# Grouping a head's softmax transpositions by key block instead of by query tile

## The chip, the cores and the metric

The kernel runs on one core of one Trainium2 chip. The metric is the device time of one execution in microseconds (us), lower is better; the times shown are a median of three runs. Engines: PE is TensorE's matmul side and PEld its weight loads, DVE is VectorE, ACT is ScalarE, POOL is GpSimd, SP is SyncE, which issues the DMAs.

## What is computed

A fused layer in three parts: a causal attention with a position bias (4 batches of 8 heads, 576 tokens, head width 64), a token mix with a two-layer ReLU network over it, and a second attention with 4 experts as heads (per batch), whose rows are gated by the two best experts. The change touches only what both attentions share, the way from the softmax matrix to its product with the values:

```
scores = where(causal, -1e9, scale * q @ k.T + min(bias, 0))
attn   = exp(scores - max);  attn = attn / (sum(attn) + 1e-9)
out    = attn @ v
```

## The kernel before

A head's 576 queries are cut into five **query tiles** t = 0 to 4 of 64, 128, 128, 128, 128 rows; because of the causal mask, tile t needs 64 + 128t keys (widths 64, 192, 320, 448, 576). In units of 128 keys, tile t has t full **key blocks** and one **diagonal half** of 64 keys. The softmax matrix of a head lies in a buffer P (two, used in turn by even and odd heads), its transposed form in a buffer pt (three, in turn).

The class `Attn` does both attentions. Its `run` (line 438) is a pipeline of **slots**, one per head and tile: slot i does, in this order, `qk` (PE: scores of tile i%5 of head i//5), `tr` (PE: transpositions of the head two before), `peak` (DVE: mask, negate, row extreme, PSUM to P; line 373), `exp` of the slot before (ACT; line 380), `evac` (ACT or DVE: the transposed pieces from PSUM to pt; lines 76 and 78, inside the helper `cp`), in every second slot of a head `norm` of the head before (DVE sums and reciprocals, lines 385 and 386, then POOL scales the five tiles of P in place, one instruction a tile, line 391), then a step of the product with the values (`pv`, line 432, once for each pair of heads, in the second slot after a pair's last `tr`, that is in slot 1 of an even head), and fillers: loads, conversions of weights, matmuls of the next stage.

So the transpositions of head n stand in the slots of head n+2, which overwrites the same buffer P. A group of transpositions r = 0 to 4 fills one PSUM bank (tag `t`, two banks), and the copy out of it must be done before the bank's next use, two groups later. `TRP` (line 67) says what group r holds: r = 0 is tile 1's key block and the diagonal halves of tiles 0 and 1; r = 1 is tile 2 with its half; r = 2 tile 3 with its half; r = 3 the four full blocks of tile 4; r = 4 its half. `evac` copies a group's full blocks by one instruction (scattered over t places of pt) and its halves by another: eight copies a head. `ENGA` and `ENGG` name the engine of each group, a for ACT and v for DVE: in the first attention r = 0 of even heads and r = 2 of odd heads go to DVE, in the second r = 4 of all heads, the others to ACT.

In the first attention (32 heads) the order on every engine is the program's; in the second (16 heads, counted from 0 again in names, 32 to 47 in the text) the framework's scheduler orders the instructions by its own estimates.

The first attention's operands L and R are loaded and split for each pair of heads while the pair before runs: `prep_steps` (line 580) splits the raw q and k into high and low parts on ACT and DVE (lines 489 and 492), and SP then issues DMAs that place the parts (line 462); the second low part is made in slot 2 of an even head, behind `peak` on DVE.

```
for i in slots:
    qk(i); tr(i - 10); peak(i); exp(i - 1); evac(i - 10)
    if i % 5 == 1: norm(i // 5 - 1)
    one step of pv; fillers(i)
```

Of the kernel before, what the change touches and what calls it, by code (L numbers as in the profile page):

```python
# [20 lines left out]
P = 128  # L21
NP = H // 2
NT = 5
# [6 lines left out]
I0 = [0, 64, 192, 320, 448]  # L30
WID = [64, 192, 320, 448, 576]
OFF = [0, 64, 256, 576, 1024]
# [4 lines left out]
PST = 448  # L37
# [12 lines left out]
STREAM = (((0, 0),), ((-1, 5),), ((0, 1),), ((0, 2), (1, -2)), ((-1, 6),), ((0, 3),), ((0, 4), (2, -3)), ((1, -1),))  # L50
FAST = (40, 70)

ENGA = ('vaaaaa', 'aavaav')
ULA = "gvgg"
WLE = "g"

HALVES = 152
UFIRST = 161
WIDE = (7,)
ENGG = ('aaaava', 'aaaava')  # L60

GTAB = "kkkkvvvvvqqqq......."
GATE = (9, 5, 2)
OB = "avava"
XG = 0

TRP = ((1, 0, 2), (2, 2, 3), (3, 3, 4), (4, 0, 0), (0, 4, 5))
HIENG = "av"
BG = (1, 1, 0, 2, 1)
ULF = "vggg"  # L70
# [3 lines left out]
def cp(nc, eng, out, in_):  # L74
    if eng == "a":
        nc.scalar.activation(out=out, in_=in_, func=AF.Copy)  # L76
    else:
        nc.vector.tensor_copy(out=out, in_=in_)


def free_ap(ap, off, dims):

    return bass.AP(tensor=ap.tensor, offset=ap.offset + off, ap=[list(ap.ap[0])] + [list(d) for d in dims])
# [76 lines left out]
def fused_kernel(ctx, tc, qk, v, s, u, vv, w12, wp, out):  # L160
    nc = tc.nc
    cst = ctx.enter_context(tc.tile_pool(name="cst", bufs=1))

    ident = cst.tile([P, P], F32, name="ident")
# [162 lines left out]
    class Attn:  # L327
# [65 lines left out]

        def tr(self, n, r):

            ps = self.pst.tile([P, 512], F32, tag="t", name=f"t_{n}_{r}")
            Pn = self.P[n % 2]
            t, a, e = TRP[r]  # L400
            for kb in range(t):
                c0 = OFF[t] + P * kb
                nc.tensor.transpose(ps[:, P * kb:P * kb + P], Pn[:, c0:c0 + P], ident)  # L403
            for k in range(a, e):
                c0, x = OFF[k] + WID[k] - 64, P * (t + k - a)
                nc.tensor.transpose(ps[0:64, x:x + P], Pn[:, c0:c0 + 64], ident)  # L406
            return ps

        def evac(self, n, r, ps):
            pt = self.pt[n % 3]  # L410
            t, a, e = TRP[r]
            if t:
                cp(nc, self.engines[n % 2][r], free_ap(pt[:, :], I0[t], [[PST, t], [1, P]]), ps[:, :P * t])
            if e > a:
                cp(nc, self.engines[n % 2][r], free_ap(pt[0:64], (PST + P) * a, [[PST + P, e - a], [1, 64]]),
                   free_ap(ps[0:64], P * t + 64, [[P, e - a], [1, 64]]))

        def push_pv(self, n):

# [90 lines left out]
    with ExitStack() as cx:  # L510
# [19 lines left out]

        attn = Attn((st, psq, pst), 4, ENGA)
        NH = B * H
# [387 lines left out]
    with ExitStack() as cx:  # L920
# [17 lines left out]

        attn = Attn((st, psq, pst), 4, ENGG)

# [162 lines left out]
        for n in range(B * E):  # L1103
            b, e = divmod(n, E)
# [105 lines left out]
```

## Time and profile before

| what | value |
|---|---|
| times of three runs | 869.67, 871.74, 872.11 us |
| median | 871.74 us |
| span of the profiled execution (first to last instruction) | 870.1 us |
| PE busy | 814.2 us, 94% of the span |
| DVE busy | 603.4 us, 69% |
| ACT busy | 466.9 us, 54% |
| POOL busy | 310.6 us, 36% |
| copies of transposed pieces | 304 on ACT, 80 on DVE |

The profile gives the span of the profiled execution and no other time of it; the median lies 1.6 us above that span. The first attention runs from about 10 to 307 us, the ReLU network from then to about 690 us, the second attention from there to the end. A duration in the profile is that of one instruction from start to end; two instructions of one engine can overlap at their ends. `x2` in a timeline row means that two instructions in a row were merged into one row.

### The profile page before, as it was taken

To read this page: it belongs to the slowest core of one execution; us is meant where nothing else is said; L and a number is where in the kernel's file an instruction comes from. 1 tells how busy PE (TensorE), PEld (TensorE's weight loads), DVE (VectorE), ACT (ScalarE), POOL (GpSimd) and SP (SyncE) were. 2 spreads that over 40 slices of the span, in tenths; PEclk is the share of its full clock that TensorE was granted. 3 is DMA by queue.
4 is the path that set the end of the run, shared out by engine and by line. 5 is a ranking of instruction groups with operands and counts; after the bars stand their busy time and mean duration, and the time that the engine had idled before them with its cause. 6 is when DMAs were issued, how large, how long until landed. Compare 5 with 4: busy or idle time off the path is not lost.

```text
span 870.1 us, 17626 instructions
## 1 busy us (share of the span) xinstructions
PE 814.2 (94%) x6068; PEld 747.8 (86%) x6068; DVE 603.4 (69%) x1759; ACT 466.9 (54%) x1384; POOL 310.6 (36%) x468
## 2 busy tenths in 40 slices
PE   3887898999999999999999999999999999999997
PEld 2665676898987889999999999999999988999875
DVE  8687788877687349985885887577446785656541
ACT  6587668866677344323442443333323567666672
POOL 5444255444334324323432342233233123232241
PEclk9898899999999999999999999999999999999999
DMA  7888479687570151111111121112000122112221
GB/s 206 224 212 213 127 187 241 165 210 194 157 195 16 56 188 37 49 50 25 53 48 48 49 61 50 49 43 57 1 1 1 30 42 43 37 55 50 67 64 61
DMA packets 36945, 79.66 MB, mean 92 GB/s; under 512 B 4792, under 2 KB 7992, under 8 KB 36856
## 3 DMA queue, kind: packets, MB, share of 16 engines
q1 hardware_dynamic: 36856, 78.53, 33.7%
q8 instruction: 48, 0.79, 0.4%
q14 instruction: 41, 0.34, 0.1%
HBM read 38.80 MB, written 8.40 MB: 54 GB/s over the span
## 4 chain that ended last, share of the span: by engine, by line
PE 72%; DVE 13%; ACT 5%; DMA 4%; issue 3%; POOL 1%; SPq 1%; DVEq 0%; POOLq 0%; ACTq 0%
PE hps L826 18%; PE facc L844 17%; PE pv L432 9%; PE qkp L1054 5%; PE t L403 4%; PE ops L1077 3%; PE facc L308 3%; PE vps L987 3%; PE qk L362 3%; PE qk L363 2%; PE hps L294 2%; DVE P L373 2%; PE t L406 2%; DMA c_raw_w<-in_w_dram 2%; DMA L<-Cd 2%
## 5 line engine op out<-in xcount | busy, mean ns | idle before, releaser
L278 POOL TENSOR_TENSOR ul<-uT,uh 128x288 fp32r<-128x288 f32 x126 | 103.8, 843 | 175.5 <-ACT uh L277 158.9
L380 ACT ACTIVATE P<-P,stat 64x64 f32<-64x64 f32 (+4 forms) x240 | 133.8, 558 | 43.4 <-DVE stat L373 39.8
L391 POOL TENSOR_SCALAR P<-P,stat 64x64 f32<-64x64 f32 (+4 forms) x160 | 100.9, 646 | 132.0 <-DVE stat L386 88.0
L373 DVE CUSTOM_DVE_ANT_0 P<-qk,mask 64x64 f32<-64x64 f32 (+4 forms) x240 | 116.4, 486 | 45.6 <-PE qk L363 28.8
L362 PE MATMUL qk<-R,L 128*128 128x288 f32 (+4 forms) x288 | 96.7, 340 | 23.1 <-DVE L L573 9.8
L830 ACT ACTIVATE hh<-hps 128x288 fp32r<-128x288 f32 x110 | 44.9, 408 | 135.2 <-PE hps L826 135.0
L76 ACT ACTIVATE pt<-t 64x64 f32<-64x64 f32 (+5 forms) x304 | 89.9, 336 | 42.0 <-PE t L406 36.6
L844 PE MATMUL facc<-hh,wh 128*128 128x288 f32 x376 | 111.2, 296 | 0.6 <-DVE aT L851 0.6
L826 PE MATMUL hps<-uh,wl 128*128 128x288 f32 x376 | 111.2, 296 | 0.0
L826 PE MATMUL hps<-ul,wh 128*128 128x288 f32 x376 | 111.1, 296 | 0.0
L826 PE MATMUL hps<-uh,wh 128*128 128x288 f32 x376 | 111.0, 295 | 0.0
L831 DVE SCALAR_TENSOR_TENSOR hl<-hps,hh 128x288 fp32r<-128x288 f32 x110 | 50.1, 455 | 87.7 <-ACT hh L830 87.4
L844 PE MATMUL facc<-hh,wl 128*128 128x288 f32 x376 | 110.9, 295 | 0.0
L844 PE MATMUL facc<-hl,wh 128*128 128x288 f32 x376 | 110.8, 295 | 0.0
L403 PE MATMUL t<-ident,P 128*128 128x128 f32 x480 | 89.6, 286 | 15.6 <-ACT pt L76 5.6
L363 PE MATMUL qk<-R,L 68*128 68x288 f32 (+9 forms) x288 | 89.1, 315 | 1.2 <-DMA L<-Cd 1.2
L391 POOL TENSOR_SCALAR P<-P,stat,pt 64x64 f32<-64x64 f32 (+4 forms) x80 | 48.5, 620 | 113.3 <-DVE stat L386 57.6
L362 PEld LDWEIGHTS qk<-R,L 128*128 128x128 f32 x288 | 57.3, 199 | 31.3 <-issue 14.9
L403 PEld LDWEIGHTS t<-ident,P 128*128 128x128 f32 x480 | 58.7, 143 | 28.9 <-issue 15.6
L432 PE MATMUL pv<-pt,V 128*64 128x288 f32 (+4 forms) x752 | 80.6, 364 | 0.0
L201 POOL TENSOR_TENSOR wl<-c_a_w,wh 128x256 fp32r<-128x256 f32 x56 | 43.6, 778 | 93.4 <-ACT wh L198 90.9
L432 PEld LDWEIGHTS pv<-pt,V 128*64 128x64 f32 x752 | 52.2, 147 | 27.8 <-issue 7.7
(194 smaller groups left out, 2196.7 us busy)
## 6 DMA issues: line engine op xcount, KB each, us to landing
c_raw_w<-in_w_dram SPq DMA_DIRECT2D x64, 256.0 KB
uT<-in_qk_dram SPq DMA_DIRECT2D x15, 576.0 KB
L<-HI SPq DMA_DIRECT2D x28, 288.0 KB
R<-HI SPq DMA_DIRECT2D x28, 288.0 KB
V<-in_v_dram SPq DMA_DIRECT2D x16, 320.0 KB
R<-uT SPq DMA_DIRECT2D x14, 288.0 KB
L<-uT SPq DMA_DIRECT2D x14, 288.0 KB
aD<-stage SPq DMA_DIRECT2D x6, 576.0 KB
```

Source lines behind the costliest of these rows:

```text
L76: nc.scalar.activation(out=out, in_=in_, func=AF.Copy)
L278: eng.tensor_tensor(out=l_, in0=src, in1=h_.bitcast(F32), op=OP.subtract)
L362: nc.tensor.matmul(ps[:, bk, :w], lhsT=q1[:, rows], rhs=k1[:, c0:c0 + w], start=True, stop=False)
L363: nc.tensor.matmul(ps[:, bk, :w], lhsT=q2[:, rows], rhs=k2[:, c0:c0 + w], start=False, stop=True)
L373: nc.vector.tensor_tensor_reduce(out=po, in0=view, in1=mk, scale=-1.0, scalar=3.0e38, op0=OP.add, op1=OP.min, accum_out=stat[P - M:, 0, t: ...
L380: nc.scalar.activation(out=po, in_=po, func=AF.Exp, scale=-1.0, bias=stat[P - M:, 0, t:t + 1], accum_out=stat[P - M:, 1, t:t + 1])
L391: nc.gpsimd.tensor_scalar(out=pv, in0=pv, scalar1=stat[r0:, 2, t:t + 1], scalar2=1.0 if gate is None else gate(t)[r0:], op0=OP.mult, op1=O ...
L403: nc.tensor.transpose(ps[:, P * kb:P * kb + P], Pn[:, c0:c0 + P], ident)
L432: nc.tensor.matmul(ps[64 * hh:64 * hh + 64, half, lo - a:e - a], lhsT=V(hh, kb), rhs=pt[:, PST * kb + lo:PST * kb + e], start=kb == 0, sto ...
L826: nc.tensor.matmul(ps, lhsT=w[:, 0, cs], rhs=x, start=i == 0, stop=i == 11)
L831: nc.vector.scalar_tensor_tensor(out=hl, in0=ps, scalar=0.0, in1=hh.bitcast(F32), op0=OP.max, op1=OP.subtract)
L844: nc.tensor.matmul(accs[c][d], lhsT=w[:, 1, cs], rhs=x, start=f == fs[0] and i == 0, stop=f == fs[-1] and i == 2)
```

## The change

The groups are cut the other way. Group 0 is now the five diagonal halves, group r = 1 to 4 is key block r-1 of the tiles r to 4: 4, 3, 2 and 1 transpositions. In pt a key block's columns of the tiles behind the diagonal lie side by side, so each group leaves PSUM by one copy with one unbroken run (512, 384, 256 and 128 columns), and group 0 by one copy of 5 times 64 columns on 64 partitions. The engine of group r is the same as before. The number of transpositions of a head is the same, 15; a group has 5, 4, 3, 2, 1 of them where it had 3, 3, 4, 4, 1.

```diff
-ENGA = ('vaaaaa', 'aavaav')
+ENGA = ('vaaaa', 'aavaa')
-ENGG = ('aaaava', 'aaaava')
+ENGG = ('aaaav', 'aaaav')
-TRP = ((1, 0, 2), (2, 2, 3), (3, 3, 4), (4, 0, 0), (0, 4, 5))
...
         def tr(self, n, r):
             ps = self.pst.tile([P, 512], F32, tag="t", name=f"t_{n}_{r}")
             Pn = self.P[n % 2]
-            t, a, e = TRP[r]
-            for kb in range(t):
-                c0 = OFF[t] + P * kb
-                nc.tensor.transpose(ps[:, P * kb:P * kb + P], Pn[:, c0:c0 + P], ident)
-            for k in range(a, e):
-                c0, x = OFF[k] + WID[k] - 64, P * (t + k - a)
-                nc.tensor.transpose(ps[0:64, x:x + P], Pn[:, c0:c0 + 64], ident)
+            if r == 0:
+                for k in reversed(range(NT)):
+                    c0 = OFF[k] + WID[k] - 64
+                    nc.tensor.transpose(ps[0:64, 64 * k:64 * k + P], Pn[:, c0:c0 + 64], ident)
+            else:
+                for t in range(r, NT):
+                    c0, x = OFF[t] + P * (r - 1), P * (t - r)
+                    nc.tensor.transpose(ps[:, x:x + P], Pn[:, c0:c0 + P], ident)
             return ps
 
         def evac(self, n, r, ps):
             pt = self.pt[n % 3]
-            t, a, e = TRP[r]
-            if t:
-                cp(nc, self.engines[n % 2][r], free_ap(pt[:, :], I0[t], [[PST, t], [1, P]]), ps[:, :P * t])
-            if e > a:
-                cp(nc, self.engines[n % 2][r], free_ap(pt[0:64], (PST + P) * a, [[PST + P, e - a], [1, 64]]),
-                   free_ap(ps[0:64], P * t + 64, [[P, e - a], [1, 64]]))
+            eng = self.engines[n % 2][r]
+            if r == 0:
+                cp(nc, eng, free_ap(pt[0:64], 0, [[PST + P, NT], [1, 64]]),
+                   free_ap(ps[0:64], 64, [[64, NT], [1, 64]]))
+            else:
+                w, c0 = P * (NT - r), (PST + P) * (r - 1) + 64
+                cp(nc, eng, pt[:, c0:c0 + w], ps[:, :w])
```

How this moves the instructions, at three places. In the names, `t_14_0` is group 0 of head 14, `qk_16_1` the scores of tile 1 of head 16, `pv_13` the product of heads 12 and 13; a row without a count is one instruction. In the changed kernel a line behind the table at line 67 has a number lower by one.

PE in the first attention, slots 0 and 1 of head 16, up to the first matmul of the pair's product; before:

```order
L362 MATMUL qk_16_0_1678<-R1_0_121,L1_0_119 128x64
L363 MATMUL qk_16_0_1678<-R2_0_124,L2_0_122 128x64
L403 MATMUL t_14_0_1681<-ident_58,P0_114 128x128
L406 MATMUL t_14_0_1681<-ident_58,P0_114 64x128 x2
L362 MATMUL qk_16_1_1695<-R1_0_121,L1_0_119 128x192
L363 MATMUL qk_16_1_1695<-R2_0_124,L2_0_122 128x192
L403 MATMUL t_14_1_1698<-ident_58,P0_114 128x128 x2
L406 MATMUL t_14_1_1698<-ident_58,P0_114 64x128
L432 MATMUL pv_13_1713<-pt0_105,V_6_1388 64x288
```

and with the change:

```order
L361 MATMUL qk_16_0_1636<-R1_0_121,L1_0_119 128x64
L362 MATMUL qk_16_0_1636<-R2_0_124,L2_0_122 128x64
L400 MATMUL t_14_0_1639<-ident_58,P0_114 64x128 x5
L361 MATMUL qk_16_1_1654<-R1_0_121,L1_0_119 128x192
L362 MATMUL qk_16_1_1654<-R2_0_124,L2_0_122 128x192
L404 MATMUL t_14_1_1657<-ident_58,P0_114 128x128 x4
L431 MATMUL pv_13_1672<-pt0_105,V_6_1356 64x288
```

Nine transpositions stand ahead of the product where six stood; group 0 reads all five tiles of P where it read tiles 0 and 1.

PE behind the product, slots 2 and 3 of the same head; before:

```order
L362 MATMUL qk_16_2_1732<-R1_0_121,L1_0_119 128x320
L363 MATMUL qk_16_2_1732<-R2_0_124,L2_0_122 128x320
L403 MATMUL t_14_2_1735<-ident_58,P0_114 128x128 x3
L406 MATMUL t_14_2_1735<-ident_58,P0_114 64x128
L362 MATMUL qk_16_3_1748<-R1_0_121,L1_0_119 128x448
L363 MATMUL qk_16_3_1748<-R2_0_124,L2_0_122 128x448
L403 MATMUL t_14_3_1751<-ident_58,P0_114 128x128 x4
```

and with the change:

```order
L361 MATMUL qk_16_2_1691<-R1_0_121,L1_0_119 128x320
L362 MATMUL qk_16_2_1691<-R2_0_124,L2_0_122 128x320
L404 MATMUL t_14_2_1694<-ident_58,P0_114 128x128 x3
L361 MATMUL qk_16_3_1705<-R1_0_121,L1_0_119 128x448
L362 MATMUL qk_16_3_1705<-R2_0_124,L2_0_122 128x448
L404 MATMUL t_14_3_1708<-ident_58,P0_114 128x128 x2
```

One transposition fewer in slot 2, two fewer in slot 3. Tile 2 of P, which `peak` of `qk_16_2` overwrites, is last read by group 2 now, in the same slot; before it was last read by group 1.

DVE in the second attention, slots 0 to 3 of head 45 (`qk_13`), with the sum and the reciprocal for head 44's `norm` (`stat0`); before:

```order
L373 ISA P1_8993,stat1_8987<-qk_13_0_10898,mask_63 64x64
L373 ISA stat1_8987 64x1
L373 ISA P1_8993,stat1_8987<-qk_13_1_10909,mask_63 128x192
L373 ISA stat1_8987 128x1
L373 ISA P1_8993,stat1_8987<-qk_13_2_10927,mask_63 128x320
L373 ISA stat1_8987 128x1
L385 TENSOR_SCALAR stat0_8985<-stat0_8985 128x5
L373 ISA P1_8993,stat1_8987<-qk_13_3_10939,mask_63 128x448
L373 ISA stat1_8987 128x1
L386 RECIPROCAL stat0_8985<-stat0_8985 128x5
```

and with the change:

```order
L372 ISA P1_8897,stat1_8891<-qk_13_0_10769,mask_63 64x64
L372 ISA stat1_8891 64x1
L384 TENSOR_SCALAR stat0_8889<-stat0_8889 128x5
L372 ISA P1_8897,stat1_8891<-qk_13_1_10781,mask_63 128x192
L372 ISA stat1_8891 128x1
L385 RECIPROCAL stat0_8889<-stat0_8889 128x5
L372 ISA P1_8897,stat1_8891<-qk_13_2_10799,mask_63 128x320
L372 ISA stat1_8891 128x1
L372 ISA P1_8897,stat1_8891<-qk_13_3_10809,mask_63 128x448
L372 ISA stat1_8891 128x1
```

The scheduler now puts the reciprocal ahead of the scores of tiles 2 and 3; at the same place of head 35, for head 34, its order is the same as before.

## Rows read from the trace of the kernel before

**Rows 1.** Engines by stage: stretch, length, busy us (instructions) by engine, PEclk, DMA share, GB/s.

```profile
10.00:160.00 150.00, 124.07 (x838) 97.04 (x839) 122.00 (x408) 112.16 (x358) 69.70 (x105) 0.92 0.78 201
160.00:295.00 135.00, 131.34 (x1047) 117.37 (x1047) 100.13 (x325) 90.17 (x283) 55.55 (x86) 1.00 0.54 145
...
690.00:725.00 35.00, 32.27 (x244) 29.56 (x244) 26.96 (x104) 24.20 (x76) 11.71 (x20) 1.00 0.17 35
725.00:820.00 95.00, 94.83 (x742) 86.62 (x739) 56.43 (x199) 61.58 (x184) 26.49 (x48) 1.00 0.20 51
820.00:870.00 50.00, 43.07 (x291) 33.48 (x289) 18.09 (x60) 26.59 (x82) 12.48 (x22) 1.00 0.20 60
```

**Rows 2.** Chain of waits, first attention, three places: start us, length us, what.

```profile
58.35 5.94 DMA L<-uT
...
133.14 4.19 DMA L<-Cd
...
138.59 2.92 PE pv L432 x32
...
142.86 0.45 PE t L403 x4
...
146.31 4.34 DMA L<-Cd
...
150.74 0.27 PE qk L363
```

**Rows 3.** Timeline of DVE, slot 2 of head 16; in brackets idle time before, releaser.

```profile
142.15 0.49 DVE L373 CUSTOM_DVE_ANT_0 P<-qk,mask 128x320 f32<-128x320 f32 x1 [0.65 <-POOL P L391]
...
142.56 0.83 DVE L492 SCALAR_TENSOR_TENSOR uT<-uT,half,HI 128x576 fp32r<-128x576 f32 x1
```

**Rows 4.** Copies out of PSUM, by form (busy us, mean ns) and from timelines.

```profile
L76 ACT ACTIVATE pt<-t 128x512 f32<-128x512 f32 x48 | 28.1, 586 | 4.2 <-PE t L403 4.1
...
L76 ACT ACTIVATE pt<-t 128x384 f32<-128x384 f32 x32 | 15.6, 487 | 31.6 <-PE t L406 31.5
...
155.81 0.59 ACT L76 ACTIVATE pt<-t 128x384 f32<-128x384 f32 x2 [0.52 <-PE t L406]
...
L78 DVE COPY pt<-t 128x384 f32<-128x384 f32 x16 | 8.8, 551 | 3.4 <-PE t L406 3.4
...
77.93 0.68 DVE L78 COPY pt<-t 128x384 f32<-128x384 f32 x2
```

**Rows 5.** Timelines: POOL's five scalings and PE's group 0, of heads 4, 14, 34, 44.

```profile
48.81 2.90 POOL L391 TENSOR_SCALAR P<-P,stat 64x64 f32<-64x64 f32 x5 [6.36 <-ACT pt L76]
...
50.46 0.30 PE L403 MATMUL t<-ident,P 128*128 128x128 f32 x1
...
134.81 3.12 POOL L391 TENSOR_SCALAR P<-P,stat 64x64 f32<-64x64 f32 x5 [2.85 <-DVE stat L386]
...
137.51 0.33 PE L403 MATMUL t<-ident,P 128*128 128x128 f32 x1
...
717.98 3.10 POOL L391 TENSOR_SCALAR P<-P,stat,pt 64x64 f32<-64x64 f32 x5 [8.20 <-ACT pt L76]
...
720.30 0.30 PE L403 MATMUL t<-ident,P 128*128 128x128 f32 x1 [0.82 <-POOL P L391]
...
828.12 3.10 POOL L391 TENSOR_SCALAR P<-P,stat,pt 64x64 f32<-64x64 f32 x5 [9.55 <-DVE stat L386]
...
829.76 0.30 PE L403 MATMUL t<-ident,P 128*128 128x128 f32 x1 [0.82 <-POOL P L391]
```

**Rows 6.** Timeline of DVE: scores of tile 3 of head 45, ahead of head 44's reciprocal.

```profile
827.13 0.63 DVE L373 CUSTOM_DVE_ANT_0 P<-qk,mask 128x448 f32<-128x448 f32 x1 [0.18 <-PE qk L363]
```

**Rows 7.** Two stretches of Rows 1's view, and the product that the chain has there.

```profile
70.00:80.00 10.00, 7.42 (x56) 6.07 (x53) 8.61 (x30) 7.64 (x25) 5.54 (x10) 1.00 0.98 260
80.00:90.00 10.00, 7.95 (x48) 5.17 (x47) 5.54 (x20) 4.44 (x15) 4.81 (x8) 0.66 0.68 170
...
83.45 5.53 PE pv L432 x32
```

## The prediction

> **What bounds the kernel now.** First the stretches [rows 1], to see which engine is full in which stage. In the second attention between 725 and 820 us PE works 94.83 of 95 us, in the first attention between 160 and 295 us 131.34 of 135: there PE sets the time, and copies on ACT (61.58 and 90.17 us) lie beside it. From 10 to 160 us nobody is full: PE 124 of 150, DVE 122, ACT 112. So there I read the chain of waits. Three times it goes the same way [rows 2]: the pair's product (138.59 us, 2.92 us long), the scores and transpositions behind it, then a DMA that brings the operands of the next pair (146.31, 4.34 us), then the first scores of that pair (150.74), which waited for it; the other two such DMAs are those at 58.35 and 133.14. What joins product and DMA is on DVE [rows 3]: the scores of tile 2 come at 142.15 after 0.65 us of idling, and the split whose result the DMA carries stands right behind them, at 142.56. The row puts the idling down to POOL, but POOL's scaling of that buffer had ended at 134.81 + 3.12 = 137.93 [rows 5]; the chain has PE there. So in this stretch a pair of heads pays for whatever stands on PE ahead of the scores of slot 2.
>
> The sum is made against the profiled execution, whose span is 870.1 us; the median of the three runs is 871.74, and a difference is carried over to it. A measurement here tells 0.3%, 2.6 us, from no change.
>
> **The copies that go.** 48 heads lose three copies each; 16 even and 16 odd heads of the first attention lose two on ACT and one on DVE, 16 of the second three on ACT: 112 on ACT, 32 on DVE. What one is worth is less than its length, since it starts before the one ahead of it ends. On ACT the pair of 384 and 64 columns takes 0.59 us; one copy of 448 columns would lie between 487 and 586 ns, about 537 [rows 4]: 0.05 us saved, 112 x 0.05 = 5.6 us of ACT. On DVE the pair takes 0.68, the 384 columns left of it 0.551: 0.13 us in each odd head; in even heads a copy of 128 and one of 2 x 64 columns become one of 5 x 64, which I take for even. That is 2 x 2 x 0.05 + 0.13 = 0.33 us for a pair of heads. From 160 to 295 us and from 725 to 820 us PE covers it: nothing. From 10 to 160 us there are about 8.5 pairs: 2.8 us if all of it were on the path, 0 if none; since chain pieces of PE and DMA hold most of that path I take 1.0. In the last two heads, which PE no longer covers (43.07 of 50 us) [rows 1], 6 x 0.05 = 0.3. **Together -1.3 us, bounds -3.1 and 0.**
>
> The Trainium skill (Perfetto Trace Analysis, Optimizing Scalar/DVE Operations) says that an instruction of these engines carries some 51 ns (ScalarE) or 125 ns (VectorE) of access to PSUM, and that grouping pays where the engine is saturated. The ACT figure agrees with the 0.05 us above; by the page's figures an estimate of what is freed is 112 x 0.051 + 32 x 0.125 = 9.7 us of engine time. Whether it pays is the second half of the rule, and by rows 1 no ACT or DVE is full; were they the bound, the third rival below would be the forecast.
>
> **The transpositions that come earlier.** Their number stays, so PE's work stays. But nine instead of six stand ahead of the product and of the scores of slot 2. Four take 0.45 us [rows 2], 0.11 each, so product and scores come 0.33 us later; by slot 4 this is made up. And DVE's step on tile 2 now also waits for the first transposition of group 2, the last reader of that piece of P, 0.11 to 0.2 us more, I take 0.15. Together 0.48 us, and on the path in the three pairs whose chain I described: **+1.4 us**. Bounds: 0, if the next DMA hides it, and 8 x 0.48 = 3.8, if every early pair pays.
>
> **The wait that comes new.** Group 0 needs tile 4's diagonal half, and so all five scalings by POOL; before, it needed two. Later groups gain that slack back, but nobody starts before group 0. I compared the end of the fifth scaling with the start of group 0 in all 48 heads; most have slack, and the cases on which this term rests are in rows 5. Head 4: 48.81 + 2.90 = 51.71 against 50.46, so 1.25 us of waiting, of which 0.35 goes into a wait that PE had anyway before group 1: 0.9. Head 14: 137.93 against 137.51, 0.42. Both stand ahead of a product of the described chain, with the scores of slot 2, the evacuation of group 0 and DVE's step on tile 0 (which overwrites what group 0 reads last) queued behind. In the second attention head 34: 721.08 against 720.30, 0.8 us, on a PE that waits there already (0.82 us) and is full from then on, so it is lost. Head 44: 831.22 against 829.76, 1.46; but there the scheduler moves the reciprocal ahead of the scores that cost 0.63 us plus 0.18 of waiting [rows 6] and of those of tile 2, so the scalings should start earlier by about as much: 0, bound 1.5. **Together +2.1 us, bounds 0 and 3.6.**
>
> **The sum:** -1.3 + 1.4 + 2.1 = +2.2 us, 870.1 + 2.2 = 872.3 of span, 871.7 + 2.2 = **873.9** as a median. All bounds together reach from -3.1 to +7.4.
>
> **Rivals.** (a) *No change, 871.7.* Early delays of PE vanish in waits that stand there anyway, since no engine is full; for it speaks that PE idles 26 of 150 us. Against it: the waits are those of a closed loop from pair to pair, which the chain shows through PE. (b) *Faster, 868.7.* DVE (122 of 150 us) is the real limit from 10 to 160 us with ACT behind it; then 0.33 us a pair come through, 2.8 us, and 0.3 at the end, and PE, running ahead, loses nothing by waiting for POOL. It decides where DVE has no idle time ahead of its score steps; rows 3 with 0.65 us speak against it for three pairs, and in other pairs the chain does stay on DVE for some us at a time. (c) *A further stretch of slow clock, 876.5.* From 70 to 80 us PE is busy 7.42 of 10 us at a granted clock of 1.00 (2.4 GHz); in the next 10 us it is 0.66, part of it at 1.2 GHz, and the product there takes 5.53 us where it takes 2.92 elsewhere [rows 7, 2]: 2.6 us for one more such place. Waits bunched ahead of group 0 could bring it about; one fewer such stretch would give the same back.
>
> The Trainium skill (TensorE: Matmul & The Clock Gate, Part 1) holds that the slow clock is the resting state and that activity releases it. By that rule, which rows 7 agree with, a new wait on PE costs more than its length, and an estimate of the price is the one just given. It speaks against this change in the early stretch.
>
> **How the numbers follow.** The forecast gets 0.40, spread from about 0 to +5, a little over half of it beyond +2.6; (a) 0.20; (b) 0.30, three quarters of it beyond -2.6, since with it one slow stretch can go too; (c) 0.10. Faster: 0.23 + 0.01 = 0.24. Slower: 0.22 + 0.10 + 0.01 = 0.33. Within 0.3%: 0.43. The range goes from 867.5, a little under (b), to 878.5, a little over (c); the forecast's own range is 871.5 to 877.
>
> **What would show it.** 192 copies on ACT and 48 on DVE. Right: PE's idle time ahead of group 0 put down to POOL's line 391 at heads 4 and 14 and 0.8 us longer at head 34; products 0.3 us later behind the first scores of their pair; ACT about 5 us less busy. From 160 to 295 and 725 to 820 us nothing changes. Wrong: a first attention that is shorter by 2 us or more, which would mean that copies, not PE's order, set the early pairs; a wait of 1.5 us at head 44; or a different number of slow-clock stretches, which would outweigh every term here.

## The result, and the profile after

The changed kernel takes **876.95 us** (median of five runs, 876.43 to 879.7) against 871.74 for the kernel before: a ratio of 1.0076, 95% interval 1.0057 to 1.0094, so 5 to 8 us slower. The forecast was 873.9, with a range of 867.5 to 878.5. The direction of the sum was right; the loss is more than twice the 2.2 us that it came to.

The profiled execution's span is 874.8 us, 4.7 more than before. The stretches, with the columns of [rows 1]:

```profile
10.00:160.00 150.00, 120.58 (x836) 96.84 (x836) 123.22 (x389) 110.37 (x322) 70.28 (x105) 0.94 0.77 200
160.00:295.00 135.00, 130.96 (x1034) 117.27 (x1033) 100.16 (x311) 89.27 (x259) 55.12 (x86) 0.99 0.53 143
690.00:725.00 35.00, 31.71 (x231) 29.36 (x230) 27.28 (x112) 24.88 (x71) 10.41 (x18) 0.97 0.17 36
725.00:820.00 95.00, 95.00 (x738) 86.69 (x738) 55.26 (x196) 60.90 (x159) 26.66 (x48) 0.99 0.20 51
820.00:870.00 50.00, 46.77 (x323) 37.21 (x319) 20.65 (x64) 26.80 (x70) 13.43 (x25) 1.00 0.16 50
```

No engine has become full that was not full before. What differs is the granted clock: 0.99, 0.97 and 0.99 in three stretches that had 1.00, and 0.94 in the first, which had 0.92. The last stretch has more PE work because everything arrives there later.

The copies by form answer to [rows 4] (line 75 is ACT's copy, 77 DVE's):

```profile
L75 ACT ACTIVATE pt<-t 128x512 f32<-128x512 f32 x48 | 28.7, 598 | 5.9 <-PE t L404 4.6 <-ACT pt L75 0.3
...
L75 ACT ACTIVATE pt<-t 64x320 f32<-64x320 f32 x32 | 13.5, 421 | 4.1 <-PE t L400 3.8
...
L77 DVE COPY pt<-t 128x384 f32<-128x384 f32 x16 | 8.8, 552 | 3.1 <-PE t L404 3.1
L77 DVE COPY pt<-t 64x320 f32<-64x320 f32 x16 | 7.7, 483 | 0.5
```

There are 240 copies where there were 384, as the change says. ACT's busy time fell from 466.9 to 463.6 us; DVE's rose from 603.4 to 605.6.

The scalings and group 0, which answer to [rows 5] (POOL's line is now 390, group 0 is line 400, the other groups 404), of heads 4, 34 and 44 in this order, and ahead of them group 0 of head 1:

```profile
29.91 1.00 PE L400 MATMUL t<-ident,P 128*64 128x128 f32 x5 [2.14 <-POOL P L390]
...
48.64 0.33 POOL L390 TENSOR_SCALAR P<-P,stat 64x64 f32<-64x64 f32 x1 [5.05 <-DVE stat L385]
49.12 2.56 POOL L390 TENSOR_SCALAR P<-P,stat 128x192 f32<-128x192 f32 x4 [0.15 <-POOL P L390]
...
51.73 0.73 PE L400 MATMUL t<-ident,P 128*64 128x128 f32 x5 [1.18 <-POOL P L390]
...
719.59 3.10 POOL L390 TENSOR_SCALAR P<-P,stat,pt 64x64 f32<-64x64 f32 x5 [7.90 <-PE qk L362]
...
722.74 0.92 PE L400 MATMUL t<-ident,P 128*64 128x128 f32 x5 [1.71 <-POOL P L390]
723.45 1.06 PE L404 MATMUL t<-ident,P 128*128 128x128 f32 x4
...
831.05 3.10 POOL L390 TENSOR_SCALAR P<-P,stat,pt 64x64 f32<-64x64 f32 x5 [8.48 <-PE t L404]
...
834.21 0.74 PE L400 MATMUL t<-ident,P 128*64 128x128 f32 x5 [1.72 <-POOL P L390]
```

Group 0 of heads 4, 34 and 44 starts 0.05 or 0.06 us behind the end of the fifth scaling. At heads 34 and 44 PE waits 1.71 and 1.72 us where it waited 0.82 [rows 5]. Head 1's is the longest of the new waits, and no term of the sum has it; heads 3 to 6 start between 0.1 us earlier and 0.8 us later than before, so little of its 2.14 us shows there. Behind head 34 the four transpositions of group 1 take 1.06 us; four took 0.45 [rows 2].

The rows of the kernel before put its 0.82 us down to POOL, too, but that wait was for something else. The second scaling of head 34, the last that group 0 needed there, ran from 718.48 to 718.99 us, and group 0 started at 720.30, 0.15 us behind the end of ACT's copy of 512 columns:

```profile
719.57 0.58 ACT L76 ACTIVATE pt<-t 128x512 f32<-128x512 f32 x1
```

That copy empties group 3 of the head before, two groups earlier, and so frees the bank. At head 44 it is the same: the second scaling ended at 829.13, the copy at 829.61, and group 0 started at 829.76. The change made a wait for a bank into a longer one for POOL.

The slow transpositions behind head 34 are the half clock. The granted clock (third column from the right) around head 34, and at 213 us, in the changed kernel:

```profile
210.00:220.00 10.00, 7.99 (x50) 7.66 (x49) 5.32 (x16) 4.63 (x14) 4.38 (x6) 0.83 1.00 240
720.00:725.00 5.00, 2.78 (x14) 1.77 (x12) 1.96 (x7) 3.75 (x12) 4.01 (x7) 0.81 0.13 27
```

and in the kernel before:

```profile
720.00:725.00 5.00, 4.70 (x39) 3.83 (x41) 1.45 (x8) 3.20 (x12) 3.79 (x7) 1.00 0.00 0
```

PE was busy 2.78 of these 5 us in place of 4.70, and part of them ran at 1.2 GHz in place of 2.4.

To see where the time goes, take the start of the first scores of a head and subtract the start of the same scores in the kernel before. Up to head 23 the difference swings between -2.9 and +1.9 us. It is +0.6 at head 24, +1.9 at head 34 (most of that arises at the half clock around 215 us), +4.2 at head 37, behind head 34's group 0, and +4.4 at head 47, behind head 44's.

### The profile page after: what moved, and what is told of

It reads as the page before. It is cut to its first block, busy times and chain, and to the rows that moved or that the text cites. A ratio compares the mean times of both kernels' runs of the same rounds, so it can differ in the third digit from the quotient of the medians.

```text
span 874.8 us, 17325 instructions
## 1 busy us (share of the span) xinstructions
PE 813.9 (93%) x6068; PEld 751.2 (86%) x6068; DVE 605.6 (69%) x1727; ACT 463.6 (53%) x1272; POOL 310.6 (36%) x468
## 4 chain that ended last, share of the span: by engine, by line
PE 73%; DVE 13%; DMA 5%; ACT 4%; issue 3%; POOL 1%; SPq 0%; DVEq 0%; ACTq 0%; POOLq 0%
PE facc L843 17%; PE hps L825 17%; PE pv L431 8%; PE qkp L1053 5%; PE t L404 4%; PE facc L307 3%; PE ops L1076 3%; PE hps L293 3%; PE qk L361 3%; PE qk L362 3%; PE vps L986 3%; PE t L400 2%; DVE P L372 2%; DMA c_raw_w<-in_w_dram 2%; POOL P L390 1%
## 5 line engine op out<-in xcount | busy, mean ns | idle before, releaser
L372 DVE CUSTOM_DVE_ANT_0 P<-qk,mask 64x64 f32<-64x64 f32 (+4 forms) x240 | 116.6, 487 | 47.1 <-PE t L404 23.5
L75 ACT ACTIVATE pt<-t 64x320 f32<-64x320 f32 (+1 forms) x192 | 84.1, 439 | 39.0 <-PE t L404 32.5
L404 PEld LDWEIGHTS t<-ident,P 128*128 128x128 f32 x480 | 60.5, 147 | 22.6 <-ACT pt L75 14.9
L431 PE MATMUL pv<-pt,V 128*64 128x288 f32 (+4 forms) x752 | 76.2, 348 | 0.2 <-DVE stat L372 0.2
L843 PEld LDWEIGHTS facc<-hh,wh 128*128 128x128 f32 x376 | 70.6, 188 | 1.0 <-issue 0.9
```

Of the source, the lines that this page charges most:

```text
L372: nc.vector.tensor_tensor_reduce(out=po, in0=view, in1=mk, scale=-1.0, scalar=3.0e38, op0=OP.add, op1=OP.min, accum_out=stat[P - M:, 0, t: ...
L404: nc.tensor.transpose(ps[:, x:x + P], Pn[:, c0:c0 + P], ident)
L431: nc.tensor.matmul(ps[64 * hh:64 * hh + 64, half, lo - a:e - a], lhsT=V(hh, kb), rhs=pt[:, PST * kb + lo:PST * kb + e], start=kb == 0, sto ...
L843: nc.tensor.matmul(accs[c][d], lhsT=w[:, 1, cs], rhs=x, start=f == fs[0] and i == 0, stop=f == fs[-1] and i == 2)
```

## The experiments

Four theories. **Theory 1**: group 0 waits for POOL's fifth scaling, and the half clock that follows such a wait on PE adds to it. **Theory 2**: PE's order, nine transpositions in place of six ahead of the product and of the scores of slot 2. **Theory 3**: chance, the half clock falling differently from run to run. **Theory 4**, formed during the study: DVE's scores of a tile overwrite what the transpositions of the same slot read, and so wait for them. All were timed beside the kernel before, whose median in these comparisons was 871.9 to 872.8 us.

The differences in the profiles, us at the start of a head's first scores, less the kernel before; the first column of numbers is the time at half clock ahead of head 24:

```
                          half clock  head 24     34      37      45      47
kernel before                23.9        0        0       0       0       0
changed kernel               17.1       0.60    1.90    4.17    3.72    4.41
changed kernel again         20.5       1.01    1.20    3.45    3.01    5.35
new groups, 1st att. only    23.9       1.92    2.08    2.07    2.08    2.08
changed, DVE scales tile 4   27.3       3.57    3.30    3.58    3.08    2.84
before, order 2 3 4 0 1      13.7      -3.39   -3.39   -2.88   -2.87    2.85
same, 1st att. only          13.7      -1.61   -1.74   -1.71   -1.52   -1.55
by tile, 1st att. only       13.7       0.10   -0.42   -0.41   -0.40   -0.39
shifted, 1st att. only       17.1      -3.77   -3.96   -3.93   -3.94   -3.96
shifted, both                17.1      -2.62   -4.07   -3.41   -4.03   -4.22
```

**The changed kernel again.**

> The changed kernel once more, for its profile. If the stretches of half clock at about 215 and 723 us follow from the waits there (theory 1), they come again at the same places, and the times are within 1 us of 877. If they are chance (theory 3), they fall elsewhere in this execution and the span moves by 1 to 3 us.

877.38 us (875.42 to 880.49, six runs), ratio 1.0066 (1.0046 to 1.0087). The waits come again to 0.01 us:

```profile
722.04 1.18 PE L400 MATMUL t<-ident,P 128*64 128x128 f32 x5 [1.70 <-POOL P L390]
...
833.49 0.73 PE L400 MATMUL t<-ident,P 128*64 128x128 f32 x5 [1.71 <-POOL P L390]
```

The half clock behind head 34 comes again; the one at 215 us does not, and there is one behind head 44 in its place:

```profile
210.00:220.00 10.00, 8.01 (x61) 7.69 (x61) 6.10 (x18) 5.24 (x16) 4.58 (x6) 1.00 0.97 229
720.00:725.00 5.00, 3.29 (x12) 1.95 (x12) 1.49 (x7) 3.21 (x9) 4.08 (x7) 0.72 0.01 3
832.00:842.00 10.00, 8.51 (x54) 5.95 (x55) 2.65 (x12) 4.92 (x14) 4.66 (x8) 0.83 0.12 25
```

So the waits are the kernel's; which of them is followed by half clock differs from one execution to the next. Theory 3 explains the spread, not the loss.

**The wait alone, in both attentions.**

```diff
-            for t in range(NT):
+            for t in (2, 3, 4, 0, 1):
```

> The kernel before, with one edit: POOL scales the tiles of a head in the order 2, 3, 4, 0, 1 in place of 0 to 4, so that the first group of transpositions (tiles 0 and 1) has to wait for all five scalings, as the diagonal halves do in the changed kernel; transpositions, copies and their order stay. Theory 1 (the loss is the wait of group 0 for the fifth scaling, and what queues behind it): the waits of the changed kernel come back, about 1.7 us ahead of group 0 of heads 34 and 44 in place of 0.8, and the time is 3 to 6 us over the kernel before, 875 to 878 us. Theory 2 (the loss is PE's order, nine transpositions in place of six ahead of the product and of the scores of slot 2): within 1 us of the kernel before.

877.16 us (873.3 to 880.9, nine runs), ratio 1.0064 (1.0042 to 1.0086): as much as the whole change. Group 0 (which begins with line 403 here) of heads 34 and 44:

```profile
717.43 0.33 PE L403 MATMUL t<-ident,P 128*128 128x128 f32 x1 [1.66 <-POOL P L391]
...
828.33 0.47 PE L403 MATMUL t<-ident,P 128*128 128x128 f32 x1 [2.20 <-POOL P L391]
```

The profile has nearly all of the loss in one place. At head 34 the wait costs 0.5 us (-3.39 to -2.88 in the table), with the clock at 1.00 behind it. At head 44 it goes with half clock, and 5.7 us are lost:

```profile
820.00:840.00 20.00, 16.85 (x91) 11.99 (x90) 6.71 (x27) 10.02 (x35) 6.50 (x12) 0.74 0.15 31
```

Ahead of head 24 nothing is lost in it. So the wait alone can cost the second attention as much as theory 1 says; the first needed a run of its own.

**The wait alone, in the first attention.**

```diff
-            for t in range(NT):
+            for t in (2, 3, 4, 0, 1) if self.engines is ENGA else range(NT):
```

> The kernel before, with POOL's scalings in the order 2, 3, 4, 0, 1 in the first attention alone (heads 0 to 31): there group 0 waits for all five scalings, and nothing else changes. The new grouping costs about 2.6 us in the first attention. If that is the wait of group 0 (theory 1): 874 to 876 us. If it is the order of work on PE and what DVE's scores then wait for (theories 2 and 4), the wait alone costs little there: 869 to 872.5 us; the profile of the same edit in both attentions had head 24 3.4 us earlier than the kernel before, though with 10 us less of half clock ahead of it.

872.92 us (12 runs), ratio 1.0003 (0.9984 to 1.0022). The waits are there, the longest at head 1 (1.38 us), then at heads 4 and 8; together they are 2.9 us, where the two profiles of the changed kernel have 3.7 and 2.9 in the first attention:

```profile
50.90 0.33 PE L403 MATMUL t<-ident,P 128*128 128x128 f32 x1 [1.05 <-POOL P L391]
...
79.31 0.33 PE L403 MATMUL t<-ident,P 128*128 128x128 f32 x1 [0.48 <-POOL P L391]
```

and they cost 0.3 us by the ratio, at most 1.9 by the interval. So theory 1 is not what costs the first attention most of its loss; a part of it is not excluded.

**The new groups in the first attention only.**

```diff
+            if self.engines is ENGA:
                 (groups and copies of the changed kernel)
+            else:
+                (groups and copies of the kernel before)
```

> The new grouping in the first attention alone (heads 0 to 31); the second attention keeps the groups and copies of the kernel before. By the starts of the heads in two profiles of the changed kernel, 1.2 to 2.1 us of the loss lie ahead of head 32 and the rest, 3 to 4 us, behind it. Theory 1 with these places: 872.5 to 874.5 us. If the loss is one of the first attention, 876 us or more; if that part was chance, 872.

874.37 us (12 runs), ratio 1.0032 (1.0018 to 1.0045), within what was expected. So the first attention costs 1.6 to 3.9 us, and the second the rest: 3.1 and 3.3 us by the medians of the two comparisons of the changed kernel, each less its own kernel before, 3.0 and 3.8 by the ratios. In the table the line is flat behind head 24: with the old groups the second attention loses nothing.

**The wait taken away in the second attention, and its control.**

```diff
-                nc.gpsimd.tensor_scalar(out=pv, in0=pv, scalar1=stat[r0:, 2, t:t + 1],
+                eng = nc.vector if self.engines is ENGG and t == 4 else nc.gpsimd
+                eng.tensor_scalar(out=pv, in0=pv, scalar1=stat[r0:, 2, t:t + 1],
```

> The changed kernel, with the scaling of tile 4 (128 x 576) on DVE in place of POOL in the second attention; POOL keeps tiles 0 to 3 there, and the first attention is untouched. By columns tile 4 is about a third of POOL's 3.1 us. Theory 1 (PE waits ahead of group 0 for POOL's fifth scaling): the waits of 1.7 us ahead of group 0 of heads 34 and 44 fall to 0.8 or less, and the second attention gives back 2 to 4 us (the wait and the half clock behind it): 873 to 875 us. Theory 2 (PE's order) or theory 4 (DVE's scores wait for the transpositions of the same slot): no gain, or a loss for the additional work on DVE, 876.5 us or more.

874.89 us (12 runs), ratio 1.0036 (1.0022 to 1.005): 2.1 to 2.5 us less than the two medians of the changed kernel, 2.6 to 3.5 by the ratios. At head 34 POOL's four scalings and DVE's one run side by side, and PE waits 0.48 us for a copy and 0.40 for POOL:

```profile
721.22 2.57 POOL L391 TENSOR_SCALAR P<-P,stat,pt 64x64 f32<-64x64 f32 x4 [8.58 <-PE qk L362]
...
721.05 0.58 DVE L391 TENSOR_SCALAR P<-P,stat,pt 128x576 f32<-128x576 f32 x1
...
723.14 0.30 PE L401 MATMUL t<-ident,P 128*64 128x128 f32 x1 [0.48 <-ACT pt L75]
...
723.84 0.63 PE L401 MATMUL t<-ident,P 128*64 128x128 f32 x4 [0.40 <-POOL P L391]
...
832.73 0.63 PE L401 MATMUL t<-ident,P 128*64 128x128 f32 x4 [0.20 <-POOL P L391]
```

In the table the step from head 34 to 37 is +0.28, where it was +2.27 and +2.25; the step from 45 to 47 is -0.24, where it was +0.69 and +2.34. What stays is the first attention.

> The control to the run before: the same move of tile 4's scaling to DVE in the second attention, in the kernel before, whose group 0 does not read tile 4. Theory 1: within 1 us of the kernel before, 871 to 873 us (its waits of 0.8 us at heads 34 and 44 are for the scaling of tile 1, which starts no earlier). If the move by itself is worth 2 us or more here too, then what it gives the changed kernel is not the wait of group 0.

871.53 us (12 runs), ratio 0.9992 (0.9979 to 1.0006). By itself the move is worth 0.7 us, and at most 1.8 by the interval, so most of what it gave the changed kernel is group 0's wait. The waits ahead of group 0 stay in the control, 0.81 and 0.82 us at heads 34 and 44, and the rows now name ACT's copy: the expectation had them as waits for the scaling of tile 1, which they are not. Together with the flat line of the run before, this shows theory 1 for the second attention.

**PE's order: two misses.**

```diff
 (tr, groups 1 to 4)
-                for t in range(r, NT):
-                    c0, x = OFF[t] + P * (r - 1), P * (t - r)
-                    nc.tensor.transpose(ps[:, x:x + P], Pn[:, c0:c0 + P], ident)
+                for kb in range(r):
+                    c0 = OFF[r] + P * kb
+                    nc.tensor.transpose(ps[:, P * kb:P * kb + P], Pn[:, c0:c0 + P], ident)
 (evac, groups 1 to 4)
-                cp(nc, eng, pt[:, c0:c0 + w], ps[:, :w])
+                cp(nc, eng, free_ap(pt[:, :], I0[r], [[PST, r], [1, P]]), ps[:, :P * r])
```

> The changed kernel, with group 0 as it is (five diagonal halves, one copy) and the other four groups by tile again: group r holds the r full blocks of tile r. Still five copies a head and the same wait for five scalings, but five and one transpositions stand ahead of the product, six as in the kernel before, and DVE's scores of tiles 2 to 4 have to wait for the whole group of the same slot. Theory 1 (the wait for the fifth scaling): 875.5 to 878 us, no better than the changed kernel by more than 1 us. Theory 2 (PE's order): it gives back 1.4 us or more, below 875.5 us, and the waits of 1.7 us at heads 34 and 44 may stay.

880.06 us (875.91 to 881.45), ratio 1.0086 (1.0061 to 1.011): slower than both theories said. Its profile has more half clock everywhere (mean granted clock 0.972) and loses from head 34 on what the changed kernel loses and more. The gain of 1.4 us that theory 2 wanted did not come. But the run mixes two attentions with different limits, and in either it changes more than the count.

```diff
 (run, ahead of tr)
+                first = len(self.pvq) == 2
+                if first:
+                    self.pvq.pop(0)()
 ...
-                if self.pvq:
+                if self.pvq and not first:
                     self.pvq.pop(0)()
```

> The changed kernel, with the product of a pair moved ahead of the transpositions of its slot (slot 1) on PE: only the five halves stand ahead of it, fewer than in the kernel before; all else stays. Theory 1: within 1.5 us of the changed kernel (876 to 878). Theory 2: it falls by 1.4 us or more, to 875.5 or below, with the products 0.4 us earlier behind the first scores of their pair.

886.37 us, ratio 1.0169 (1.0143 to 1.0194): 9 us slower than the changed kernel, where theory 2 wanted a gain. What the product was moved past now waits for it. DVE's scores, in the changed kernel:

```profile
L372 DVE CUSTOM_DVE_ANT_0 P<-qk,mask 64x64 f32<-64x64 f32 (+4 forms) x240 | 116.6, 487 | 47.1 <-PE t L404 23.5 <-PE t L400 10.2 <-PE qk L362 7.0
```

and here:

```profile
L372 DVE CUSTOM_DVE_ANT_0 P<-qk,mask 64x64 f32<-64x64 f32 (+4 forms) x240 | 116.5, 487 | 74.3 <-PE t L404 53.6 <-PE t L400 11.5 <-PE qk L362 5.5
```

53.6 us of waiting for transpositions in place of 23.5: the scores of tile 1 overwrite what group 1 reads, and group 1 now stands behind a product of 2 to 3 us. This run gave theory 4.

**Theory 4 by itself, in the first attention.**

```diff
-TRP = ((1, 0, 2), (2, 2, 3), (3, 3, 4), (4, 0, 0), (0, 4, 5))
+TRPA = ((0, 0, 2), (1, 2, 3), (2, 3, 4), (3, 4, 5), (4, 0, 0))
-ENGA = ('vaaaaa', 'aavaav')
+ENGA = ('vaaaa', 'aaava')
 ...
 (tr and evac read TRPA in the first attention, TRP in the second)
```

> The kernel before, with the groups of the first attention shifted by a slot: group 0 holds the halves of tiles 0 and 1, group r the r full blocks of tile r, and the half of tile r + 1. Eight copies a head and the wait for two scalings stay, and four transpositions in place of six stand ahead of the product; but DVE's scores of a tile, which overwrite what these transpositions read, now wait for the group of the same slot, as they do in the changed kernel. Theory 4 (DVE's scores behind the transpositions of the same slot): 873.5 to 876 us. Theory 2 (PE's order ahead of the product): 869.5 to 872. Theory 1 (POOL's fifth scaling): 871 to 873, no difference.

869.33 us (868.22 to 869.85), ratio 0.9961 (0.9946 to 0.9977): **faster** than the kernel before, 3.4 us by the medians beside each other. DVE's scores do wait for the same slot's transpositions, as theory 4 says. Their row here, then that of the kernel before, then that of the run with the new groups in the first attention only:

```profile
L374 DVE CUSTOM_DVE_ANT_0 P<-qk,mask 64x64 f32<-64x64 f32 (+4 forms) x240 | 116.6, 487 | 46.0 <-PE qk L364 18.4 <-PE t L407 13.5 <-PE t L404 7.3
...
L373 DVE CUSTOM_DVE_ANT_0 P<-qk,mask 64x64 f32<-64x64 f32 (+4 forms) x240 | 116.4, 486 | 45.6 <-PE qk L363 28.8 <-PE t L406 11.5 <-POOL P L391 2.8
...
L373 DVE CUSTOM_DVE_ANT_0 P<-qk,mask 64x64 f32<-64x64 f32 (+4 forms) x240 | 116.5, 487 | 52.0 <-PE qk L363 20.5 <-PE t L406 12.1 <-PE t L402 8.5
```

(The first figure behind the second bar is all of the idle time, the others are its largest parts.) Their idle time, 46.0 us, is hardly more than in the kernel before, 45.6 us, and the time is less. So a wait for the same slot's group does not by itself make the kernel slower. That the larger groups of the new grouping, behind which the scores idle 52.0 us, cost something in this way is not excluded. The direction is that of theory 2: four transpositions ahead of the product, and 3.4 us less. The edit also moves 16 copies from DVE to ACT, so the count is not its only difference.

**The count back from nine to six, with the new group 0, in the first attention.** The edit of the by-tile groups above, under the switch of the run with the first attention only. The sizes of the other groups change with it: DVE's copy in odd heads has 256 columns in place of 384, 0.42 us in place of 0.55.

> As the run with the new grouping in the first attention alone (874.4 us), but with groups 1 to 4 by tile: group 0 holds the five halves, group r the r full blocks of tile r. Five copies a head, the wait for all five scalings and DVE's wait for the same slot are those of the new grouping; only the count of transpositions ahead of the product and of the scores of slot 2 goes back from nine to six, that of the kernel before. Theory 2 (PE's order): 2 us or more are given back, 870 to 872.5 us. If the half of tile 4 in group 0, the merged copies or DVE's waits cost the first attention its 2.6 us: 873.5 to 876.

873.67 us (12 runs), ratio 1.0015 (1.0001 to 1.0029), between what the two sides expected. Against 1.0032 (1.0018 to 1.0045) with nine, half of the loss seems to come back, but the intervals overlap: not settled.

**One slot earlier for the scalings.**

```diff
-                if i % NT == 1 and 1 < i <= n + 1:
+                if i % NT == 0 and 1 < i <= n + 1:
                     self.norm(i // NT - 1)
```

> The changed kernel, with a head's reciprocal and its five scalings issued one slot earlier (behind the last exponential of the head, and so ahead of the scores of slot 1 on DVE in place of behind them). Theory 1: the scalings start some 0.6 us earlier (one score step of DVE), the waits ahead of group 0 shrink by as much, and the time falls by 1 to 4 us, to 873 to 876. Against it: DVE then waits in the reciprocal for the exponential of tile 4, with the scores of slot 1 queued behind it, and the time stays or rises, 877 to 880.

884.51 us, ratio 1.0135 (1.0115 to 1.0156): a miss in the direction named "against it". DVE's idle time ahead of the step with the sums (which feeds the reciprocal), by what ended it (us, times), here:

```profile
L384 DVE TENSOR_SCALAR stat<-stat x48: 149/170/171, 16.8 to 858.6; 128x5 f32<-128x5 f32 x48
its engine sat idle before it (us, times) until:
  ACT P L379: 14.9, 22
```

and in the changed kernel:

```profile
L384 DVE TENSOR_SCALAR stat<-stat x48: 158/165/809, 17.1 to 852.5; 128x5 f32<-128x5 f32 x48
its engine sat idle before it (us, times) until:
  ACT P L379: 4.9, 8
```

DVE stands 10 us longer in front of ACT's exponentials, with the scores of slot 1 queued behind. The waits ahead of group 0 at heads 34 and 44 are 1.69 and 1.71 us here, as before the edit, so that this run says nothing on theory 1.

**A version that beats both.** The shifted groups in both attentions, with `ENGG = ('vaaaa', 'vaaaa')`.

> A version meant to beat both kernels: the groups of the run that shifted them by a slot (group 0 the halves of tiles 0 and 1, group r the full blocks of tile r and the half of tile r + 1), now in both attentions. In the first attention it gave 3.4 us. In the second, group 0 still needs tiles 0 and 1 alone, so the waits at heads 34 and 44 stay at 0.8 us, and PE is full in between: 868 to 870.5 us. If DVE's scores waiting for the group of the same slot cost the second attention, where the changed kernel loses 2.6 us: 871 to 873.

**867.8 us** (866.29 to 869.89, seven runs), ratio 0.9954 (0.9936 to 0.9973). The waits at heads 34 and 44 did not stay at 0.8 us, they halved:

```profile
716.22 0.38 PE L406 MATMUL t<-ident,P 128*64 128x128 f32 x2 [0.42 <-POOL P L391]
...
824.80 0.38 PE L406 MATMUL t<-ident,P 128*64 128x128 f32 x2 [0.42 <-POOL P L391]
```

These rows, too, name POOL. But the second scaling ended at 715.40 and 824.47 us, and group 0 started 0.10 us behind the end of ACT's copies of group 3, 716.12 and 824.70: it is the wait for the bank again, with four transpositions (group 4) between where one stood. The shorter waits show no gain: from head 34 to the end the table has -0.15 us. The gain lies ahead of head 34, and the ratio is within the interval of the run that shifted the first attention alone (0.9961).

## Why the prediction was right, and where it was wrong

**Right: the sign, and the mechanism in the second attention.** The wait ahead of group 0 at head 34 was forecast at 0.8 us more than before, for POOL's fifth scaling, and measured at 0.89 (1.71 less 0.82), behind that scaling. That the 0.82 us of before were a wait for ACT's copy and not for POOL changes nothing in this sum, since group 0 starts behind whichever ends last.

**Wrong: what the waits are worth, place by place.** The term "the wait that comes new" was +2.1 us, of which 1.3 lay at heads 4 and 14 and 0.8 in the second attention. As far as the intervals tell it was the other way round. In the first attention the wait alone cost 0.3 us by the ratio (1.0003, at most 1.9 us); head 4's wait came, head 14's did not, and head 1's, the longest, was not counted, though POOL's scalings there ended at 29.05 us in the kernel before and group 0 started at 27.73. In the second attention, forecast at +0.8 for the wait and -0.3 for the copies, the change costs 3.0 to 3.8 us, for two reasons:

- *Head 44, taken as 0.* It was argued that an earlier reciprocal would take 1.46 us off the wait. POOL's scalings started at 831.05, 2.9 us later than in [rows 5], where the heads around ran 3.7 later; so 0.8 us was gained, and a wait of 1.72 was left, 0.9 more than before. The bound of 1.5 was nearer than the value taken.
- *The half clock, put into rival (c) with a chance of 0.10.* Head 34's 0.89 us turned into 2.25 to 2.27 in both profiles of the changed kernel, with half clock behind; nearly the same wait (1.66) cost 0.5 in the run with the scalings in another order, where none followed. Head 44's cost 0.7 without it and 2.3 with it. Rival (c) priced one stretch at 2.6 us for the whole place, which is about what head 34 cost. It looked for it in the early stretch and named the waits ahead of group 0 as the cause. Head 34 is another place; the cause agrees with every profile of the second attention (see the last section).

The Trainium skill (TensorE: Matmul & The Clock Gate, Part 1) holds that the slow clock is the resting state. The stretch at 720 us, with PE busy 2.78 of 5 us at a granted 0.81, agrees; the wait of 1.66 us with the clock at 1.00 behind it shows that not every such wait is answered so.

**Not settled: the first attention.** Forecast -1.0 (copies) +1.4 (transpositions) +1.3 (waits) = +1.7; measured +1.6 to +3.9. That +1.7 lies within is in part luck, since the waits alone came to 0.3. With that, copies and transpositions together come to about +2.5 by the ratios, where -1.0 and +1.4 had them at +0.4; the two intervals together leave room from about +0.5 to +4.5 (an estimate, their half-widths added as squares). Either the copies gave less than 1.0, or the transpositions cost more than 1.4; runs with fewer transpositions ahead of the product took less time (four: a ratio of 0.9961; six, with the new group 0: 1.0015; nine: 1.0032), but each differs in something else too, no run separates the two terms, and this stays open.

**The copies.** ACT was to lose 5.6 us of busy time and lost 3.3. No run shows that any of it reached the time: by the last rows of the first view PE covers it from 160 to 295 and from 725 to 820 us, as forecast. The rule weighed there, of the Trainium skill (Perfetto Trace Analysis, Optimizing Scalar/DVE Operations), goes on to say that where these engines are not full but keep others waiting, breaking instructions up may let work finish sooner. No run here shows that: the fastest kernel, 867.8 us, has eight copies a head, but so has the kernel before.

**The rivals.** (a), no change, and (b), faster, lie outside the interval. (b) wanted the relief of DVE and ACT to come through in the early stretch; the new groups made the first attention slower in place of faster. (c), at 876.5 us, came nearest. (Where the prediction weighs the rule on grouping, it points at the third rival; the one in which DVE and ACT set the time is the second, (b).)

**What was forecast to show.** 192 and 48 copies: yes. Group 0's idle time put down to POOL at head 4: yes, 1.18 us; at head 14: no. "A wait of 1.5 us at head 44" and "a different number of slow-clock stretches" stood under *wrong*, and both came. "Products 0.3 us later" came where PE is full: in heads 22 to 30 the product starts 0.27 to 0.30 us later behind the first scores of its pair than before. In the early stretch, where it was priced, the distance changes by -1.0 to +1.2 us (heads 4 to 18), which shows neither the delay nor its cost.

## What to carry to other kernels

When groups are recut, look at what the *first* group needs and not at the number of instructions: a group that reads the ends of all tiles waits for the last producer, and what is queued behind it on that engine waits too. A wait on a matmul engine that is otherwise full should be priced at its length and, as a second case of real weight, at its length plus a stretch of half clock. Before a wait is priced by the engine that its row names, look when that engine was done: the row of the 0.82 us named POOL, and it was ACT. The version that put four transpositions at the end of a head and two at its start took no more instructions and was 0.46% faster; its gain came in the first attention, and which of its differences gave it is not shown.

## What the hardware showed that was not expected

- **The price of one wait depends on the clock behind it.** Six profiles have waits of 1.66 to 2.20 us ahead of group 0 at heads 34 and 44 (changed kernel twice, order 2 3 4 0 1, by tile, product first, scalings a slot earlier). Of these twelve waits, seven go with half clock at the wait or behind it; of the sixteen in the other eight profiles, 0.9 us at most, none does. By the starts of heads 34 and 37, 45 and 47, less the kernel before, the five without it cost 0.4 to 0.7 us, four with 3.4 us of half clock 2.3 to 2.8, two with 6.8 us 3.3 and 4.3, one with 10.2 us 5.7: about 0.5 us and half the length of the stretch (an estimate from these twelve).
- **The clock carries much of the spread.** Fourteen executions of the kernel before had spans of 867.6 us at a mean granted clock of 0.994 to 872.2 at 0.986; the four at 0.986 average 871.1, so about 0.43 us for each 0.001. Five of the changed kernel average 875.8 us at 0.9834, those fourteen 870.1 at 0.9886: by that slope some 2.2 of the 5.7 us go with the clock (an estimate). The two executions of the changed kernel at 0.986 average 874.7, 3.6 us above those four.
- **The same code reaches the same head at different times.** Four profiles with the new groups in the first attention have head 24 at +0.60, +1.01, +1.92 and +3.57 us, in the order of their time at half clock ahead of it: 17.1, 20.5, 23.9 and 27.3 us. A single profile cannot tell 2 us in that stretch, and the changed kernel's first one, at +0.60, hid part of its loss there.
